# One PSUM tile with a free list, and the key steps of 15 units scored in three groups instead of four

## The chip, the cores and the metric

The kernel runs on one core of a Trainium2 chip. The metric is the device time of one execution in microseconds (us). Three runs of the kernel before took 412.25, 418.48 and 414.56 us; the median is 414.56 us. The profile is one execution of the same program, taken by the hardware profiler.

Names used below: PE is the matrix engine (TensorE), PEld its weight loads, ACT the scalar engine, DVE the vector engine, POOL the GpSimd engine, SP the engine that issues most DMAs. PSUM is the memory of eight banks into which PE writes its results; ACT and DVE read them out.

## The reference

```
q_n, k_n = rmsnorm(q, g_q), rmsnorm(k, g_k)       # 8 batches x 12 heads x 448 x 64
scores   = (q_n @ k_n^T) / 8
attn     = exp(scores - rowmax) ; attn /= rowsum + 1e-9
x        = (attn @ v) as 3584 tokens x 768
h        = x @ w_in                                # 768 x 2048
out      = max(0.01 h, h) @ w_out                  # 2048 x 768
```

## The kernel before, in words

**Units.** The attention is done in 24 units `u`; one unit is four heads of one batch, so three units make a batch. The 448 keys of a unit are cut into seven key steps of 64. For one key step `t`, `score` (line 196) issues four 64x64 matmuls with 448 columns, two for each of two PSUM banks. Such a pair of banks is a *slot* (`slot`, line 193). `ex` (line 209) then empties the slot with one ACT instruction, the exponential of 128x896 scores (line 218), into the tile `et`, from which the sums and the product with `v` are taken (`zcol`, line 299; `pv`, line 360).

**Stages of a unit.** The main loop (lines 982 to 1073) gives each unit from 3 on four stages, `d` = 0 to 3. At the start of a stage `qk` (line 202) scores the steps of `STEPS[d]`: step 0, then 1 and 2, then 3 and 4, then 5 and 6. In stage 0 there follow the row maximum on DVE (`shift_max`), the product with `v` and the sums of the unit before (`pv_slot`, `zcol`), a small matmul and DVE work that give the exponent's shift (`shift_mm`, lines 243 to 257), a copy of the product out of PSUM (`pv_out`, line 316, called `x` in the profile), and the logarithm of the sums (`zcol_ln`, line 327). `ex` comes right behind the scores in stages 1 to 3.

**Items.** The rest of each stage is filled by `fill` (line 756) with items of the two dense layers, taken from a queue. `PLAN` (line 745) says how many for each unit and stage, mostly two or three. An item `moe1` (line 385) is six matmuls of 128x128 with 448 columns into one bank `hps`, which ACT empties with the leaky ReLU (line 383). Items of the second layer (`moe2`, line 425, and `seven`, line 480) are eight matmuls of 384 columns, mostly emptied by DVE. After each item `fill` calls one of the stage's `jobs`: loads, normalisation of later units, squares for the unit three ahead (`prep_sq`, line 148, on ACT in stage 3), and the like. Each engine executes its own instructions in the order in which the program lists them (`manual_schedule`); engines wait for each other by semaphores.

**PSUM.** The eight banks are two pools: two slots of two banks (tag `sT`), and four single banks (tag `aux`) handed out in turn. `hold` and `drop` (lines 62 to 69) turn the four single banks into a list for the last two batches; in the tail two more banks join it (line 646). Slots hold the scores, the product with `v`, and some sums; single banks hold the results of items, the sums of `zcol`, and transposes.

**Ends.** Units 0 to 2 are written out by hand before the loop (lines 786 to 980), units 22 and 23 carry the last batches' items (`late1`, line 605), and a tail after the loop (lines 1074 to 1084) runs what is left in the queue.

Of the kernel before, what the change touches and what calls it, by code (L numbers as in the profile page):

```python
# [18 lines left out]
def kernel(  # L19
# [34 lines left out]

    held = []

    def aux(shape, dtype, name):
        if held:
            return held[0].pop(0)
        return psum.tile(shape, dtype, tag="aux", bufs=4, name=name)  # L60

    def hold():
        if not held:
            banks = [psum.tile([P, 512], FP32, tag="aux", bufs=4, name=f"bank{i}") for i in range(4)]
            held.append(banks)

    def drop(bank):
        if held:
            held[0].append(bank)

# [96 lines left out]
    def prep_norm(u, c=ALL, tis=BOTH):  # L167
        n = c[1] - c[0]
        for ti in tis:
# [3 lines left out]
                buf(u, "rinv")[:, ti, :, c[0]:c[1], None].broadcast_to([P, 2, n, D]), op=ALU.mult)  # L173

    def prep_tr(u, ti, copies):
        tp = aux([P, NS, P], FP16, "tp")
        for (lo, hi), copy in copies:
            for x in range(lo, hi):
                nc.tensor.transpose(tp[:, x, :], buf(u, "n16")[:, ti, x].rearrange("p a d -> p (a d)"), ident16)
            copy(buf(u, "qkT")[:, ti, lo:hi], tp[:, lo:hi], ti == 0)  # L180

    def prep_trd(u):
# [7 lines left out]
    def kT(u, r, a, t):  # L190
        return buf(u, "qkT")[64 * a:64 * a + 64, 1, t, 64 * r:64 * r + 64]

    def slot():
        return psum.tile([P, 2, 512], FP32, tag="sT", bufs=2, name="sT")

# [12 lines left out]

    def ex(u):
        s = st[u]  # L210
        if "et" not in s:
            s["et"] = epool.tile([P, NS, 2, S], FP16, tag="et", name="et")
        for t, sT in s["sT"]:
            if isinstance(sT, list):
                for a in range(2):
                    nc.scalar.activation(s["et"][:, t, a], sT[a][:, 0:S], AF.Exp, bias=s["eb"], scale=1.0)
            else:
                nc.scalar.activation(s["et"][:, t], sT[:, :, 0:S], AF.Exp, bias=s["eb"], scale=1.0)  # L218

    def score0(u):  # L220
        banks = [aux([P, 512], FP32, "s0") for a in range(2)]
        score(u, 0, banks)
        st[u]["sT"] = [(0, banks)]
# [16 lines left out]
    def shift_bank(u):  # L240
        st[u]["pb"] = aux([P, 512], FP32, "pb")

    def shift_mm(u):
        s = st[u]
        if u > 0 and "pslot" in st[u - 1]:
            pb = st[u - 1]["pslot"][:, :, S:S + 64]
            for x in range(2):
                nc.tensor.matmul(pb[:, x], onesp, s["dg"][:, 64 * x:64 * x + 64], start=True, stop=True)
            nc.vector.tensor_reduce(s["spare"][:, 510:511], pb, axis=AXL.XY, op=ALU.max)  # L249
        else:  # L250
            if "pb" not in s:
                shift_bank(u)
            pb = s["pb"]
            nc.tensor.matmul(pb[:, 0:P], onesp, s["dg"], start=True, stop=True)
            nc.vector.tensor_reduce(s["spare"][:, 510:511], pb[:, 0:P], axis=AXL.X, op=ALU.max)
        s["eb"] = small.tile([P, 1], FP32, tag="eb", name="eb")
        nc.vector.tensor_scalar(s["eb"], s["spare"][:, 510:511], -1.0, DELTA, op0=ALU.mult, op1=ALU.add)
# [41 lines left out]
    def zcol(u):  # L299
        s = st[u]  # L300
        s["zc"] = aux([P, 512], FP32, "zc")
        ets = z_tiles(u)
        for i, e in enumerate(ets):
            for y in range(2):
                for a in range(2):
                    c = 32 * (2 * y + a)
                    nc.tensor.matmul(s["zc"][c:c + 32, 0:HS], onesr, e[:, a, HS * y:HS * y + HS],  # L307
                                     start=(i == 0), stop=(i == len(ets) - 1))
# [7 lines left out]
    def pv_out(u):  # L316
        s = st[u]
        s["x32"] = zpool.tile([P, 2, S], FP32, tag="x32", name="x32")
        if u in (3, 4, 5, 6):
            nc.vector.tensor_copy(s["x32"], s["pslot"][:, :, 0:S])  # L320
        else:
            nc.scalar.copy(s["x32"], s["pslot"][:, :, 0:S])  # L322

    def zcol_ln(u):
# [24 lines left out]
    def zinv(u):  # L349
        s = st[u]  # L350
        s["rz"] = zpool.tile([P, 2, S], FP32, tag="rz", name="rz")
        if "zslot" in s:
            nc.scalar.activation(s["rz"], s["zslot"][:, :, 0:S], AF.Ln)
            nc.scalar.activation(s["rz"], s["rz"], AF.Exp, bias=0.0, scale=-1.0)
        else:
            for r in range(2):
                nc.scalar.activation(s["rz"][:, r], s["zt"][r][:, 0:S], AF.Ln)
                nc.scalar.activation(s["rz"][:, r], s["rz"][:, r], AF.Exp, bias=0.0, scale=-1.0)

    def pv(u, t0=0, t1=NS):  # L360
        s = st[u]
        if t0 == 0 and "pslot" not in s:
            s["pv"] = [aux([P, 512], FP32, "pv") for r in range(2)]
        for t in range(t0, t1):
            for r in range(2):
                for a in range(2):
                    nc.tensor.matmul(s["pv"][r][64 * a:64 * a + 64, 0:S], vts[u % NV][64 * r:64 * r + 64, a, t],  # L367
                                     s["et"][64 * r:64 * r + 64, t, a], start=(t == 0), stop=(t == NS - 1))
# [16 lines left out]
    def moe1(b, ft):  # L385
        xt = xts[b]
        hps = aux([P, 512], FP32, "hps")
        for kt in range(KT):
# [36 lines left out]
    def moe2(pair, t, half, part, late=False, cut=8):  # L425
# [3 lines left out]
        if part == 0:  # L429
            ost[1] = aux([P, 512], FP32, "op2")  # L430
        op2 = ost[1]
# [48 lines left out]
    def seven(pair, tt, nxt=None, last=False, mixed=False):  # L480
# [6 lines left out]
        def bank(name):  # L487
            g[name] = aux([P, 512], FP32, name)
            return g[name]
# [115 lines left out]
    def late1(b, tail, after):  # L605
# [32 lines left out]
        def get(n, s):  # L638
            g[n, s] = aux([P, 512], FP32, "hp")
            return g[n, s]  # L640

        def start():
            hold()
            if tail:
                for i in range(2):
                    drop(slot()[:, 0])
            for name in ("u", "v"):
# [52 lines left out]
    def push(b):  # L700
# [32 lines left out]
        else:  # L733
# [13 lines left out]
            "3232", "2222", "3323", "3232", "2322", "4356", "5232")  # L747
    STEPS = ((0,), (1, 2), (3, 4), (5, 6))

    def narrow(u):  # L750
# [35 lines left out]
    with tc.manual_schedule():  # L786
# [5 lines left out]
        load(2)  # L792
        gps = aux([P, 512], FP32, "gps")
        wbank = aux([P, 512], FP32, "warm")
        warm(32, wbank)
# [9 lines left out]
        prep_rinv(0, (0,))  # L805
        nc.vector.tensor_copy(gcol, gps[:, 0:1])
        prep_ssq(0, ALL, (1,))
        prep_rinv(0, (1,))
# [5 lines left out]
        def tr(u, ti, chunks, tp=None):  # L814
            if tp is None:
                tp = aux([P, NS, P], FP16, "tp")
            for c, copy in chunks:
                for x in range(*c):
                    nc.tensor.transpose(tp[:, x, :], buf(u, "n16")[:, ti, x].rearrange("p a d -> p (a d)"), ident16)
                copy(buf(u, "qkT")[:, ti, c[0]:c[1]], tp[:, c[0]:c[1]], ti == 0)  # L820
            return tp

        tr(0, 0, ((CA, acopy),))
        tr(0, 0, ((CB, acopy),))
        tpk = tr(0, 1, ((K0, vcopy),))
        warm(6, wbank)
        prep_sq(1, ALL, (0,))
        qk(0, STEPS[0])
        shift_max(0)
        tr(0, 1, ((K1, acopy),), tpk)  # L830
        prep_sq(1, ALL, (1,))
# [8 lines left out]
        warm(10, st[0]["pb"])  # L840
        shift_mm(0)
        prep_ssq(1)

# [19 lines left out]
        load_w_in(1024, 1024)  # L863
        wb = aux([P, 512], FP32, "warm")
        warm(12, wb)
        qk(0, (2,))
        ex(0)
        warm(8, wb)
        qk(0, (3,))
        ex(0)  # L870
        tr(1, 0, ((ALL, vcopy),))
        tpk = tr(1, 1, ((K0, vcopy),))
# [6 lines left out]
        shift_max(1)  # L879
        vcopy(*k1[0])  # L880
        shift_bank(1)
        qk(0, (5,))
# [24 lines left out]
        qk(1, (2,))  # L907
        warm(6, st[1]["pb"])
        ex(1)
        trn(2, 0, vcopy)  # L910
# [36 lines left out]
        trn(3, 0, vcopy)  # L947
        warm(8, st[2]["pb"])
        trn(3, 1, vcopy)
        xmul(1)  # L950
        prep_ssq(4, ALL, (1,))
        qk(2, (4,))
        ex(2)
        st[2]["zt"] = [aux([P, 512], FP32, "zt") for r in range(2)]
        zsum(2, 0, 3)
# [22 lines left out]
        for ft in range(2):  # L978
            prelu(0, gt[:, ft, 0:S], first[:, ft, 0:S])
        del queue[0:2]  # L980

        for u in range(3, NU):
            for d in range(4):
                if d > 0 or u > 3:
                    qk(u, STEPS[d])
                    if d == 0:
# [9 lines left out]
                        else:  # L996
# [3 lines left out]
                            zinv(u - 1)  # L1000
                    ex(u)
                    if d == 0 and narrow(u - 1):
# [7 lines left out]
                def job(fn, *args):  # L1010
                    jobs.append(lambda: fn(*args))

                if d == 0:
                    if u == 3:
# [98 lines left out]
```

## Time and profile before

| what | value |
|---|---|
| median of three runs | 414.56 us (412.25 to 418.48) |
| span of the profiled execution, first to last instruction | 410.6 us |
| its own time | not listed apart; the nearest run shown is 412.25 us, 1.6 us over the span |
| PE matmuls busy | 398.2 us (97%), 3840 |
| ACT busy | 298.4 us (73%), 470 |
| DVE busy | 307.2 us (75%), 490 |
| exponentials of one slot (line 218) | 166, 1010 ns each, 159.6 us |
| matmuls of the scores into slots (line 199) | 664 |

A line of a group or of the timeline reads: start, duration, engine, line, operation, `output<-inputs`, shape, how many. Matmuls are pipelined, so a row of twelve matmuls ends a little after the next row has begun; distances between starts are the measure. "issue" as the end of a wait means that the engine waited for nothing that the profile shows.

### The profile page before, as it was taken

Reading aid. Unit: us, or ns where it says so; the run is one execution under the profiler, and the core shown is the slowest. Engines: PE = TensorE matmul, PEld = TensorE weight load, DVE = VectorE, ACT = ScalarE, POOL = GpSimd, SP = SyncE. Lnnn points to the kernel's source line nnn. Section 1 sums busy time; section 2 is a strip of 40 time slices with the busy share of each in tenths; the row PEclk is TensorE's granted clock in tenths of the full one; section 3 lists DMA queues with packets and bytes.
Section 4 is the critical chain, followed back from the end, with each engine's and each line's share of the span. In section 5 each row is a group of like instructions: output and inputs, shape, how many; then the busy total and the mean of one; then the engine's idle time right before and its main releaser. Section 6 shows DMA issues by size and latency. Waiting matters only on the chain.

```text
span 410.6 us, 9395 instructions
## 1 busy us (share of the span) xinstructions
PE 398.2 (97%) x3840; PEld 219.7 (54%) x3840; DVE 307.2 (75%) x490; ACT 298.4 (73%) x470; POOL 69.1 (17%) x70
## 2 busy tenths in 40 slices
PE   8689999999999999999999999999999999999996
PEld 7455444454445544555445544455445557558963
DVE  5997789999788766767669667678568788658772
ACT  5998977677887699777986779967986657653600
POOL 1886433100020200020020200003001202000000
PEclk9999999999999999999999999999999999999999
DMA  5999999999565885577666896667662460032014
GB/s 192 264 255 253 232 234 236 232 190 200 136 156 95 232 224 106 149 196 169 155 151 77 216 201 143 164 127 170 196 114 46 121 152 17 7 80 77 2 44 111
DMA packets 72526, 62.87 MB, mean 153 GB/s; under 512 B 36388, under 2 KB 67620, under 8 KB 72484
## 3 DMA queue, kind: packets, MB, share of 16 engines
q1 hardware_dynamic: 61888, 50.08, 47.6%
q0 software_dynamic: 10272, 11.80, 18.4%
q8 instruction: 30, 0.49, 0.5%
q10 hardware_dynamic: 324, 0.39, 0.3%
q14 instruction: 12, 0.10, 0.1%
HBM read 45.61 MB, written 11.01 MB: 138 GB/s over the span
## 4 chain that ended last, share of the span: by engine, by line
PE 90%; DVE 4%; ACT 3%; DMA 1%; issue 1%; SPq 0%; DVEq 0%
PE hps L389 28%; PE sT L199 10%; PE sT L367 6%; PE op L435 6%; PE mc L485 5%; PE ma L485 5%; PE bank L485 5%; PE md L485 5%; PE bank L617 5%; PE zc L307 3%; PE mb L485 3%; ACT et L218 2%; PE sT L485 2%; PE bank L435 1%; DVE n L171 1%; DMA rk<-in_k_dram 1%
## 5 line engine op out<-in xcount | busy, mean ns | idle before, releaser
L218 ACT ACTIVATE et<-sT,eb 128x896 f16<-128x896 f32 x166 | 159.6, 1010 | 25.8 <-PE sT L199 13.5
L389 PE MATMUL hps<-xt,win 128*128 128x448 f16 x600 | 120.8, 353 | 0.0
L389 PEld LDWEIGHTS <-win 128*128 128x128 f16 x612 | 56.7, 98 | 57.9 <-issue 9.9
L383 ACT ACTIVATE gt<-hps 128x448 f16<-128x448 f32 x100 | 53.9, 558 | 3.8 <-PE hps L389 3.2
L199 PE MATMUL sT<-qkT 64*64 64x448 f16 x664 | 52.3, 363 | 4.0 <-ACT et L218 3.2
L159 DVE TENSOR_REDUCE ssq<-sq 128x14 f32<-128x896 f32 (+2 forms) x49 | 50.2, 1057 | 0.8 <-ACT sq L148 0.8
L485 PEld LDWEIGHTS <-sa 128*128 128x128 f16 x352 | 32.8, 98 | 26.0 <-issue 5.8
L128 POOL DMA_DIRECT2D vt<-in_v_dram x24 | 17.9, 746 | 166.4 <-PE sT L367 166.0
L322 ACT COPY x<-sT 128x896 f32<-128x896 f32 x16 | 14.5, 907 | 29.8 <-DVE sT L249 27.5
L199 PEld LDWEIGHTS <-qkT 64*64 64x64 f16 x672 | 15.4, 104 | 37.2 <-issue 32.5
L485 PEld LDWEIGHTS <-gt 128*128 128x128 f16 x264 | 25.3, 98 | 18.4 <-issue 2.1
L347 POOL TENSOR_TENSOR xt<-x,rz 128x896 f16<-128x896 f32 x9 | 19.5, 2170 | 80.8 <-DMA rz<-zs 73.5
L236 DVE TENSOR_REDUCE sT<-sT 128x1 f32<-128x896 f32 x22 | 24.1, 1096 | 11.4 <-PE sT L199 11.3
L367 PE MATMUL sT<-et,vt 64*64 64x448 f16 x560 | 29.9, 349 | 0.0
L171 DVE TENSOR_TENSOR n<-rq,rinv 128x896 f16<-128x896 f32 (+2 forms) x25 | 26.3, 1055 | 3.2 <-ACT rinv L165 3.2
L435 PE MATMUL op<-wout,gt 128*128 128x384 f16 x160 | 28.4, 327 | 0.0
L171 DVE TENSOR_TENSOR n<-rk,rinv 128x896 f16<-128x896 f32 (+2 forms) x26 | 27.5, 1065 | 0.0
L292 DVE TENSOR_TENSOR ea<-ea,et 128x896 f16<-128x896 f16 x25 | 15.6, 625 | 15.2 <-ACT et L218 14.3
L367 PEld LDWEIGHTS <-vt 64*64 64x64 f16 x672 | 20.3, 107 | 10.6 <-issue 0.4
L435 PEld LDWEIGHTS <-gt 128*128 128x128 f16 x192 | 17.7, 98 | 13.8 <-issue 3.2
L485 PE MATMUL ma<-wout,gt 128*128 128x384 f16 x128 | 23.5, 326 | 0.0
L292 DVE TENSOR_TENSOR ea<-et 128x896 f16<-128x896 f16 x14 | 9.4, 672 | 11.9 <-ACT et L218 11.9
(144 smaller groups left out, 548.4 us busy)
## 6 DMA issues: line engine op xcount, KB each, us to landing
rq<-in_q_dram SPq DMA_DIRECT2D x24, 448.0 KB, 3.9
rk<-in_k_dram SPq DMA_DIRECT2D x24, 448.0 KB, 4.9
out_dram<-ost SPq DMA_DIRECT2D x52, 192.0 KB, 3.5
rz<-zs SPq DMA_DIRECT2D x80, 112.0 KB, 2.3
vt<-in_v_dram POOLq DMA_DIRECT2D x24, 224.0 KB, 5.2
win<-in_moe_w_in_dram POOLq DMA_DIRECT2D x8, 384.0 KB, 14.3
wout<-in_moe_w_out_dram POOLq DMA_DIRECT2D x2, 1536.0 KB, 28.9
out_dram<-ost SPq DMA_DIRECT2D x4, 96.0 KB, 2.1
```

The lines of the kernel that those rows point to most:

```text
L159: nc.vector.tensor_reduce(buf(u, "ssq")[:, ti, :, c[0]:c[1]], buf(u, f"sq{ti}")[:, :, c[0]:c[1]], axis=AXL.X, op=ALU.add)
L171: nc.vector.tensor_tensor(buf(u, "n16")[:, ti, c[0]:c[1]].rearrange("p s a d -> p a s d"), src[:, :, c[0]:c[1]], buf(u, "rinv")[:, ti, :, ...
L199: nc.tensor.matmul(banks[a][64 * r:64 * r + 64, 0:S].rearrange("p (t x) -> p t x", t=NS), kT(u, r, a, t), qT(u, r, a), start=True, stop=True)
L218: nc.scalar.activation(s["et"][:, t], sT[:, :, 0:S], AF.Exp, bias=s["eb"], scale=1.0)
L236: nc.vector.tensor_reduce(s["spare"][:, 511:512], sT[:, :, 0:S], axis=AXL.XY, op=ALU.max)
L292: nc.vector.tensor_tensor(s["ea"], s["et"][:, 0] if t == 1 else s["ea"], s["et"][:, t], op=ALU.add)
L367: nc.tensor.matmul(s["pv"][r][64 * a:64 * a + 64, 0:S], vts[u % NV][64 * r:64 * r + 64, a, t], s["et"][64 * r:64 * r + 64, t, a], start=(t ...
L383: nc.scalar.activation(dst, src, AF.Prelu, bias=0.0, scale=1.0, alpha=0.01)
L389: nc.tensor.matmul(hps[:, 0:S], win16[:, kt // 2, kt % 2, ts(ft, P)], xt[:, kt // 2, kt % 2], start=(kt == 0), stop=(kt == KT - 1))
L435: nc.tensor.matmul(op2[:, 0:HC], gt[:, ft, ds(col(t), P)], wout16[:, ft, ds(HC * half, HC)], start=(i == 0), stop=(i == FT - 1))
L485: nc.tensor.matmul(bank[:, 0:HC], a[:, f], b[:, f], start=(first and f == 0), stop=(f == HF - 1), skip_group_check=not first)
L617: nc.tensor.matmul(bank[:, HX * i:HX * i + HX].rearrange("p (t x) -> p t x", t=NS), w, x[:, kt], start=start, stop=(kt == HK - 1), skip_gr ...
```

## The change

All of PSUM becomes one tile `banks` of eight banks. `aux` hands out single banks and `slot` pairs of neighbouring banks from one list `free`; `drop` gives a bank or a pair back when the program has listed its last reader, and it goes to the end of the list. Up to unit 6 the list is still parted: banks 0 to 3 single, banks 4 to 7 as two pairs. From unit 7 on (`shared`) any two free neighbours can become a slot, and `aux` takes, of all free banks but the one given back last, the first whose neighbour is in use. The same list serves the tail.

Units 7 to 21 (`tripled`) score their key steps as 0; 1, 2, 3; none; 4, 5, 6 in the four stages. `ex(u, 2)` empties the first two slots at once; the third exponential becomes the first job of the stage, so it stands behind the first item on ACT, and the stage's other jobs move back by one item. `PLAN` and the queue of items are as before.

```diff
-    held = []
-    def aux(shape, dtype, name):
-        if held:
-            return held[0].pop(0)
-        return psum.tile(shape, dtype, tag="aux", bufs=4, name=name)
...
-    def slot():
-        return psum.tile([P, 2, 512], FP32, tag="sT", bufs=2, name="sT")
+    banks = psum.tile([P, 8, 512], FP32, tag="banks", name="banks")
+    single = [banks[:, i] for i in range(8)]
+    double = [banks[:, 2 * i:2 * i + 2] for i in range(4)]
+    free = [3, 0, 2, 1, 4, 5, 6, 7]
+    shared = []
+    def mine(i):
+        return shared or i < 4
+    def aux():
+        can = [i for i in free if mine(i)]
+        if shared:
+            can = [i for i in can[:-1] if i ^ 1 not in free] or can
+        free.remove(can[0])
+        return single[can[0]]
+    def slot():
+        if shared:
+            can = [i for i in free if i ^ 1 in free]
+            last = {i // 2: n for n, i in enumerate(free) if i in can}
+        else:
+            last = {i // 2: n for n, i in enumerate(free) if i >= 4 and i ^ 1 in free}
+        x = min(last, key=lambda i: last[i])
+        for i in (2 * x, 2 * x + 1):
+            free.remove(i)
+        return double[x]
...
-    def ex(u):
+    def ex(u, most=NS):
...
-        for t, sT in s["sT"]:
+        for t, sT in s["sT"][:most]:
...
                 nc.scalar.activation(s["et"][:, t], sT[:, :, 0:S], AF.Exp, bias=s["eb"], scale=1.0)
+                drop(sT)
+        s["sT"] = s["sT"][most:]
...
+    TRIPLES = ((0,), (1, 2, 3), (), (4, 5, 6))
+    def tripled(u):
+        return 7 <= u < NU - 2
...
+                if u == 7 and d == 0:
+                    shared.append(u)
                 if d > 0 or u > 3:
-                    qk(u, STEPS[d])
+                    qk(u, (TRIPLES if tripled(u) else STEPS)[d])
...
-                    ex(u)
+                    ex(u, 2)
...
+                if st[u]["sT"]:
+                    job(ex, u)
```

The other edits put a `drop` behind each last reader (`pv_out`, `zinv`, the transposes and warm-up matmuls of the hand-written part) and call `aux()` without shape and name.

## The prediction

> **What bounds the kernel now.** I began with the busy times and the 40 slices.
>
> ```profile
> span 410.6 us, 9395 instructions
> PE 398.2 (97%) x3840; PEld 219.7 (54%) x3840; DVE 307.2 (75%) x490; ACT 298.4 (73%) x470; POOL 69.1 (17%) x70
> PEclk9999999999999999999999999999999999999999
> ```
>
> PE is busy all the way at its full granted clock; ACT and DVE have a quarter to spare. The chain that ended last lies 90% on PE. So the time goes down only if PE does less or loses less between its pieces, and goes up by whatever PE is made to wait. The waits tell which of its losses are left:
>
> ```profile
> PEld L199 <- issue: 32.5, 92, 0.8
> ...
> PE sT L199 <- ACT et L218: 3.2, 7, 0.7
> ```
>
> The scores wait for an exponential 3.2 us in all, nearly all of it in the hand-written start: from 36 us on it is one wait of 0.4 us. But 92 times a score group's first weight load stands about 0.35 us with nothing to wait for. Those are the places where PE goes from 128x128 matmuls to the 64x64 matmuls of the scores. How much of it is lost is read from the timeline; here PE in unit 10:
>
> ```profile
> 146.01 0.57 PE L199 MATMUL sT<-qkT 64*64 64x448 f16 x8
> 146.51 3.58 PE L389 MATMUL hps<-xt,win 128*128 128x448 f16 x18
> 150.02 0.57 PE L199 MATMUL sT<-qkT 64*64 64x448 f16 x8
> 150.53 2.44 PE L389 MATMUL hps<-xt,win 128*128 128x448 f16 x12
> 152.90 0.57 PE L199 MATMUL sT<-qkT 64*64 64x448 f16 x8
> 153.41 2.44 PE L389 MATMUL hps<-xt,win 128*128 128x448 f16 x12
> 155.78 0.38 PE L199 MATMUL sT<-qkT 64*64 64x448 f16 x4
> ```
>
> From item to item, 18 matmuls and a group take 150.53 - 146.51 = 4.02 us, 12 and a group 153.41 - 150.53 = 2.88. Six matmuls are thus 1.14 (0.19 each), and a group of two steps costs 2.88 - 12 x 0.19 = 0.60. A key step itself costs 0.57 - 0.38 = 0.19 (eight matmuls against four). Two steps are 0.38, so each **group loses 0.22 us** in going to 64x64 and back.
>
> **What goes.** Units 7 to 21 have one group less in stages 1 to 3 (the group of stage 0 runs straight into the product with v, also 64x64). Fifteen groups at 0.22 are **3.3 us off PE**. Its matmuls remain; so do the counts on ACT and DVE, and SP and POOL list the same instructions in the same order, so no load, store or transpose is passed by anything new on its queue. Bounds: 0 if three steps in a row cost the 0.22 in another way; 15 x 0.35 = 5.3 if all of the issue wait were lost.
>
> [...]
>
> **What is added: waits for banks.** Three steps need six of the eight banks at once. The order of the built program shows which reader each new pair waits for. Within the loop all are per bank: no wait covers the whole tile. In stage 1 the first pair waits for the copy x, the second for the exponential of step 0, as before. The third is new. It waits for the first two leaky ReLUs of stage 0 in units 7, 8, 11, 14, 17, 20; for the logarithm and the first of them in 10, 13, 16, 19; for the logarithm, with or without a DVE copy, in 9, 12, 15, 18, 21. Whether that is late is read from ACT in unit 10:
>
> ```profile
> 144.24 0.91 ACT L322 COPY x<-sT 128x896 f32<-128x896 f32 x1 [2.27 <-DVE sT L249]
> 145.04 1.01 ACT L218 ACTIVATE et<-sT,eb 128x896 f16<-128x896 f32 x1
> 145.94 0.36 ACT L327 ACTIVATE zs<-zc 128x224 f32<-128x224 f32 x1
> 146.18 0.56 ACT L383 ACTIVATE gt<-hps 128x448 f16<-128x448 f32 x1
> ```
>
> The third step would start 0.38 after the group, at 146.39; the ReLU ends at 146.74. **Units 10 and 16** (only two items in stage 0) wait 0.35, with the signal some 0.4: 0.8 us together. Behind it on PE stands everything else, so it counts in full. With three items PE comes a whole item later: in unit 11 the second ReLU ends at 161.73 and the third step would start at 161.49 + 0.38 = 161.87; unit 8: 114.98 against 115.02; unit 14: 209.37 against 209.41. Those just fit. In units 12 and 18 the logarithm ends about 0.05 late: 0.1 together.
>
> **What moves on ACT.** In stage 3 a third exponential (0.95) stands behind the first item's ReLU and ahead of the two squares (0.96 each). Everything ACT does up to the next unit's copy x ends up to 0.95 later; PE comes only 0.19 later. What covers it is the idle time ahead of that copy:
>
> ```profile
> ACT x L322 <- DVE sT L249: 27.5, 15, 3.9
> ```
>
> By unit it is 0.72 (unit 8), 2.03, 2.27, 0.38 (unit 11), 2.56, 2.27, 1.18 (unit 14), 2.31, 2.27, 0.38 (unit 17), 2.56, 2.27, 1.18, 2.03. Only 8, 11 and 17 are short: by 0.95 - 0.19 less the idle, 0.04, 0.38 and 0.38. Some of that comes back because stage 2 has no exponentials now and ACT reaches stage 3 free of queue: step 4 could begin about 0.3 earlier than the 153.70 of unit 10. I take 0.15 in each of the three, **0.45 us** (0 to 1.1). If that cover is gone, the copy, the next exponential and both ReLUs slip together, and the third step of stage 1 is what is late next.
>
> The product with v needs step 6 last. In unit 10 the third exponential would end near 156.8 and the last matmuls that read it start about 157.5: it fits by 0.7. The third group of stage 3 waits for readers of stage 2, which ACT, without exponentials there, serves at once; I take nothing (a ReLU late each time would be 0.56). Inside the stages the banks come back from the two early exponentials, one or two items ahead of need. DVE's additions of exponentials and its sums of squares shift by an item, with a stage to spare.
>
> **The tail** has eight banks instead of six, but `aux` may take a fresh one. Two items of the last batch now use the bank whose ReLU was issued two items before, where the old list gave an older one. The ReLU (`gt<-bank`) starts at 378.12 and ends at about 378.68, and the item that would now use its bank starts at 378.50: 0.25 with the signal; at 385.40 the same costs 0.2. Together **0.45 us**. Units 0 to 6, 22 and 23 keep their groups, and the readers they wait for end before PE comes: nothing.
>
> **Sum** on the profiled execution: -3.3 + 0.8 + 0.1 + 0.45 + 0.45 = -1.5, a span of 409.1 for 410.6. That execution lies 1.6 under the fastest run and 4.0 under the median; I carry the difference over to the median: 414.56 - 1.5 = **413.1 us**.
>
> **Rivals.**
> 1. *Full gain.* PE slips by the first waits, ACT catches up, and the free list spares the tail: -3.3 or, with part of the wider issue bound, -4, 410.6 to 411.3. For it: single waits of 0.04 to 0.4 are small against ACT's idle quarter. Against: the waits of units 10 and 16 come from the DVE result that starts the copy, and no slack elsewhere moves it.
> 2. *No change.* The loss recurs, for instance because the third step's matmuls don't follow without a gap, 0.22 x 15 given back: with the waits, about +1.8, or 416.4; if the waits are absent too, 414.6. Against: 28 matmuls with v in a row keep 0.19 for each four.
> 3. *Slower: ACT becomes the bound at each unit's start.* The place is the third pair of stage 1. If it waits on average half a ReLU-and-signal more than I find in all fifteen units, say 0.5 each, the cost is 7.5 + 0.45 - 3.3 = +4.7, 419.2 us. It decides from 0.2 us a unit on, where waits eat the 3.3. Beyond 2% (+8.3) it takes 0.75 a unit, that is ACT late by its whole 0.95 everywhere. For it: margins of 0.04 in units 8, 14 and 20. Against: idle of over 2 us ahead of the copy in nine of the units.
>
> **Chances.** The forecast, -3 to 0: 0.57. Full gain: 0.18. No change up to +2: 0.12. Slower by more than that: 0.13, of which 0.04 beyond 2%. Two per cent, 8.3 us, is about what a measurement of this kernel tells from no change, and a gain of that size has no source in PE's 0.22 a group: 0.02. The range leaves out most of the slower case and adds the scatter of a median of runs that lie 6 us apart: 410 to 418.
>
> **What would show it.** Right: 15 fewer score groups; groups of twelve matmuls spaced about 0.8 from item to item; the issue wait on the score loads down by some 5 us; PE's waits at score groups near 1.5 us, in units 10 and 16 above all. Wrong: PE waiting for a ReLU or an exponential in most units' stage 1 or 3, an ACT with no idle time ahead of the copy x, or a lost 0.22 that reappears inside the twelve.

## The result

| | before | after |
|---|---|---|
| median | 416.52 us (412.25 to 418.86, four runs) | 433.0 us (432.63 to 433.88, four runs) |
| ratio, with its 95% interval | | 1.0456 (1.0397 to 1.0514) |
| span of the profiled execution | 410.6 us | 431.4 us |
| its own time | not listed apart | 433.22 us, 1.8 over its span |

The ratio counts fast runs alone, so it is not the quotient of the two medians (1.040): two of the four runs before, at 418.48 and 418.86 us, took over 1.5% longer than the fastest. By it the change made the kernel slower by 4.6%; 413.1 us had been forecast. The page of the kernel after answers the first question, whether PE is still busy all the way:

```profile
span 431.4 us, 9408 instructions
...
PE 404.2 (94%) x3840; PEld 225.1 (52%) x3840; DVE 310.5 (72%) x490; ACT 300.2 (70%) x470; POOL 68.9 (16%) x70
...
PEclk9899999999979999999997999999996999999999
```

It is not. PE is idle for 6% of the span (3% before), its matmuls take 6 us longer in all although their number is the same, and the granted clock has four dents where there were none. The waits of the same kernel (engine and line, what it waited for: total us, times, longest) say who keeps it waiting. In this kernel line 222 is the score matmul, 242 the exponential, 414 the leaky ReLU, 497 and 500 the sums `s1` and `s2`, 516 the matmuls of `seven`, 538 the copy of `ma`:

```profile
PEld L222 <- issue: 29.6, 83, 0.8
...
DVE sa L497 <- ACT gt L414: 18.7, 3, 6.7
...
PE banks L516 <- DVE ost L538: 7.8, 3, 2.8
...
PE banks L516 <- DVE sa L500: 6.2, 3, 2.1
...
PE banks L222 <- ACT et L242: 3.3, 8, 0.6
```

The scores are not at fault: their issue wait fell from 32.5 to 29.6 us, and they wait 3.3 us for exponentials, nearly what they did before (3.2). What is new are three waits of about 2.1 us and three of 2.2 to 2.8 us, PE standing at `seven` for DVE. They are in three units only. To place them I took, unit by unit, the start of the first sum matmul of `zcol` (`zc<-et,onesr`, now `banks<-et,onesr`) in both timelines, and from one such mark to the next the difference, after minus before:

| stretch | difference, us |
|---|---|
| start to unit 4 | +1.26 |
| units 4 to 6 | 0.00 |
| unit 7, 9, 11, 13, 15, 17, 19, 21 | -0.22, -0.22, -0.23, -0.24, -0.24, -0.24, -0.23, -0.23 |
| units 12, 18 | -0.16, -0.17 |
| units 10, 16 | +0.21, +0.23 |
| **units 8, 14, 20** | **+6.84, +7.68, +6.53** |
| unit 22 | +0.01 |
| the rest, units 23 and tail | +0.23 |

The first row is not the change's: in the runs below the same stretch lies between +0.2 and +1.7 us, and in this one the clock is at half from 17.7 to 21.1 us, in the hand-written start. Units 8, 14 and 20 lose 21.05 us together; everything else gives back about 1.5. The whole result is in three units.

These are the units of the tripled ones that have `ADDED` equal to 3, and the loop treats them alike: stage 1 has, after the job `prep_g`, one composite job of two sums of squares (`prep_ssq`, `ssq` in the rows) and two additions of exponentials (`add_e`, `ea`). DVE in unit 8 of the kernel before (start, duration, engine, line, operation, form, count, and in brackets the idle time ahead of it and what ended that):

```profile
112.71 0.45 DVE L155 TENSOR_SCALAR qkT<-qkT,gcol 128x896 f16<-128x896 f16 x1
113.07 2.08 DVE L159 TENSOR_REDUCE ssq<-sq 128x14 f32<-128x896 f32 x2
116.34 0.62 DVE L292 TENSOR_TENSOR ea<-et 128x896 f16<-128x896 f16 x1 [1.20 <-ACT et L218]
117.24 0.62 DVE L292 TENSOR_TENSOR ea<-ea,et 128x896 f16<-128x896 f16 x1 [0.28 <-ACT et L218]
118.20 0.43 DVE L466 TENSOR_TENSOR sa<-gt 128x512 f16<-128x512 f16 x1 [0.33 <-ACT gt L383]
118.66 0.43 DVE L469 TENSOR_TENSOR sa<-sa,gt 128x512 f16<-128x512 f16 x1
119.00 0.55 DVE L507 COPY ost<-ma 128x384 f32<-128x384 f32 x1
119.47 1.85 DVE L472 TENSOR_TENSOR sa<-gt 128x512 f16<-128x512 f16 x1
```

and in the same unit of the kernel after:

```profile
113.76 0.45 DVE L176 TENSOR_SCALAR qkT<-qkT,gcol 128x896 f16<-128x896 f16 x1
120.04 2.29 DVE L497 TENSOR_TENSOR sa<-gt 128x512 f16<-128x512 f16 x1 [5.83 <-ACT gt L414]
122.36 0.43 DVE L500 TENSOR_TENSOR sa<-sa,gt 128x512 f16<-128x512 f16 x1
122.70 2.07 DVE L180 TENSOR_REDUCE ssq<-sq 128x14 f32<-128x896 f32 x2
124.69 0.62 DVE L320 TENSOR_TENSOR ea<-et 128x896 f16<-128x896 f16 x1
125.34 0.62 DVE L320 TENSOR_TENSOR ea<-ea,et 128x896 f16<-128x896 f16 x1
125.88 0.55 DVE L538 COPY ost<-banks 128x384 f32<-128x384 f32 x1
```

Three things are different. First, the order: the composite job came one place later. In unit 8 the item in between is the first of `seven`, which puts `s1` and `s2` on DVE's list; in units 14 and 20 stage 1 has only two items, and a job that is left over comes behind what the end of the stage lists, which is `s1` and `s2` again. So `ssq` and `ea`, which could have run in the 5.83 us of idle time, now stand behind `s1`, which waits for ACT, and ahead of the copy of `ma`. Second, `s1` starts late; why is on ACT:

```profile
118.07 0.60 ACT L414 ACTIVATE gt<-banks 128x448 f16<-128x448 f32 x1
118.50 1.08 ACT L242 ACTIVATE et<-banks,eb 128x896 f16<-128x896 f32 x1
119.39 0.62 ACT L414 ACTIVATE gt<-banks 128x448 f16<-128x448 f32 x1
```

The third exponential, 1.08, lies between the two leaky ReLUs of the stage, and `s1` needs the second. Third, `s1` takes 2.29 in place of 0.43. POOL runs its product of x and 1/z just then:

```profile
119.98 2.06 POOL L376 TENSOR_TENSOR xt<-x,rz 128x896 f16<-128x896 f32 x1 [7.28 <-DMA rz<-zs]
```

In the kernel before the same product fell on `s3` (the row at 119.47: 1.85 in place of 0.41), which nothing waited for. PE in the same unit shows what follows:

```profile
115.66 0.78 PE L222 MATMUL banks<-qkT 64*64 64x448 f16 x12
116.37 2.44 PE L420 MATMUL banks<-xt,win 128*128 128x448 f16 x12
118.65 1.46 PE L516 MATMUL banks<-wout,gt 128*128 128x384 f16 x8
119.95 0.81 PE L516 MATMUL banks<-tw,sa 128*128 128x384 f16 x4
122.84 0.82 PE L516 MATMUL banks<-tw,sa 128*128 128x384 f16 x4 [2.08 <-DVE sa L500]
126.49 2.72 PE L516 MATMUL banks<-wout,gt 128*128 128x384 f16 x8 [2.82 <-DVE ost L538]
129.14 1.33 PE L222 MATMUL banks<-qkT 64*64 64x448 f16 x12
```

PE waits for `s2`, then, after four matmuls, for the copy, and then its matmuls are slow: eight take 2.72 where 1.46 is usual, and twelve of the scores 1.33 in place of 0.78. By distances between starts, against the 0.65 of four matmuls, 1.39 of eight ahead of a score group and 0.70 of twelve scores that undisturbed rows have, unit 8 loses 2.24 at the first wait, 3.00 at the second and 1.82 to the slow matmuls, less the 0.22 gained: 6.84. Units 14 and 20 are split in the same way (in unit 20 the first four matmuls behind the first wait are slow too, 1.43, but the second wait covers that). Over the three: **6.7 us at the first wait, 9.0 at the second, 6.0 to the clock**, less 0.7 gained.

So far this is read, not shown. The groups of three, the new list of banks and the order of jobs all changed at once.

### The profile page after: what moved, and what is told of

Its sections match the earlier page's. It is cut to its first block, busy times and chain, and to the rows that moved or that the text cites. A ratio compares the mean times of both kernels' runs of the same rounds, so it can differ in the third digit from the quotient of the medians.

```text
span 431.4 us, 9408 instructions
## 1 busy us (share of the span) xinstructions
PE 404.2 (94%) x3840; PEld 225.1 (52%) x3840; DVE 310.5 (72%) x490; ACT 300.2 (70%) x470; POOL 68.9 (16%) x70
## 4 chain that ended last, share of the span: by engine, by line
PE 76%; ACT 10%; DVE 7%; DMA 4%; issue 1%; POOL 0%; SPq 0%; ACTq 0%; DVEq 0%; POOLq 0%
PE banks L516 22%; PE banks L420 22%; PE banks L222 8%; PE banks L466 7%; PE banks L398 6%; PE banks L648 6%; ACT et L242 6%; PE banks L335 2%; ACT gt L414 2%; DVE sa L497 2%; DMA rq<-in_q_dram 1%; DVE ssq L180 1%; DMA qkT<-n 1%; DMA rk<-in_k_dram 1%; DMA out_dram<-ost 1%
## 5 line engine op out<-in xcount | busy, mean ns | idle before, releaser
L242 ACT ACTIVATE et<-banks,eb 128x896 f16<-128x896 f32 x166 | 160.6, 1015 | 27.3 <-PE banks L222 14.8
L420 PE MATMUL banks<-xt,win 128*128 128x448 f16 x612 | 122.2, 353 | 0.0
L414 ACT ACTIVATE gt<-banks 128x448 f16<-128x448 f32 x104 | 56.8, 566 | 5.8 <-PE banks L420 4.6
L222 PE MATMUL banks<-qkT 64*64 64x448 f16 x672 | 52.7, 375 | 3.9 <-ACT et L242 3.3
L516 PE MATMUL banks<-tw,sa 128*128 128x384 f16 x264 | 48.9, 333 | 6.2 <-DVE sa L500 6.2
L523 DVE TENSOR_TENSOR ost<-banks,ost 128x384 f32<-128x384 f32 x55 | 30.5, 554 | 21.7 <-PE banks L516 20.2
L516 PE MATMUL banks<-wout,gt 128*128 128x384 f16 x176 | 36.2, 353 | 7.8 <-DVE ost L538 7.8
L516 PEld LDWEIGHTS <-gt 128*128 128x128 f16 x264 | 26.5, 102 | 28.5 <-issue 13.4
L398 PE MATMUL banks<-et,vt 64*64 64x448 f16 x672 | 37.0, 349 | 0.1
L222 PEld LDWEIGHTS <-qkT 64*64 64x64 f16 x672 | 18.1, 107 | 35.6 <-issue 29.6
L466 PE MATMUL banks<-wout,gt 128*128 128x384 f16 x192 | 34.1, 327 | 0.0
L262 DVE TENSOR_REDUCE banks<-banks 128x1 f32<-128x896 f32 x22 | 24.1, 1097 | 10.3 <-PE banks L222 10.3
```

Source lines behind the costliest of these rows:

```text
L222: nc.tensor.matmul(banks[a][64 * r:64 * r + 64, 0:S].rearrange("p (t x) -> p t x", t=NS), kT(u, r, a, t), qT(u, r, a), start=True, stop=True)
L262: nc.vector.tensor_reduce(s["spare"][:, 511:512], sT[:, :, 0:S], axis=AXL.XY, op=ALU.max)
L414: nc.scalar.activation(dst, src, AF.Prelu, bias=0.0, scale=1.0, alpha=0.01)
L420: nc.tensor.matmul(hps[:, 0:S], win16[:, kt // 2, kt % 2, ts(ft, P)], xt[:, kt // 2, kt % 2], start=(kt == 0), stop=(kt == KT - 1))
L466: nc.tensor.matmul(op2[:, 0:HC], gt[:, ft, ds(col(t), P)], wout16[:, ft, ds(HC * half, HC)], start=(i == 0), stop=(i == FT - 1))
L516: nc.tensor.matmul(bank[:, 0:HC], a[:, f], b[:, f], start=(first and f == 0), stop=(f == HF - 1), skip_group_check=not first)
```

## The experiments

The theory: the change's third exponential, put in as first job, reorders DVE in units 8, 14 and 20, and the rest follows from that. Rival A: three key steps in a row make PE wait for ACT. Rival B: the one PSUM tile with its list makes PE wait for banks. "Steps" are the differences of the table above. The ratios are to runs of the kernel before that were taken beside each experiment; their medians are 413.8 to 414.3 us.

### e1_order_back: the order on DVE restored

```diff
-                if st[u]["sT"]:
+                with_g = d == 1 and u in (8, 14, 20)
+                if st[u]["sT"] and not with_g:
                     job(ex, u)
...
-                if d == 1 and 5 <= u < NU - 1:
+                if with_g:
+                    job(lambda u: (ex(u), prep_g(u + 1)), u)
+                elif d == 1 and 5 <= u < NU - 1:
                     job(prep_g, u + 1)
```

> The changed kernel, but in stage 1 of units 8, 14 and 20 the third exponential shares one job with the scaling of q for the next unit, so that the sums of squares and the additions of exponentials stand on DVE ahead of the sums s1 and s2 again, as in the kernel before; groups, list of banks and everything else stay. Theory (the order on DVE in three units): the steps of units 8, 14 and 20, +6.8, +7.7 and +6.5 us against the kernel before, become about -0.2 each like their neighbours'; the span is near 408.5 us, or 409.7 if the clock dips at the start of the kernel again, and the ratio to the kernel before is 0.990 to 0.999. Rival A (three steps in a row make PE wait for ACT's exponentials and leaky ReLUs): the groups stay, so the loss stays, a span of 428 to 432. Rival B (PSUM as one tile with a list makes PE wait for banks): it stays too, 428 to 432.

Measured: a span of 415.4, 419.07 us, ratio 1.0116 (1.0084 to 1.0149). The steps of the three units are +2.04, +2.00 and +2.00. 15 of the 21 us are the order on DVE with the clock behind it, and both rivals lose most of their ground; but the theory's -0.2 did not come. The second wait is gone, the first is as long as ever. DVE of this kernel in unit 8:

```profile
118.98 2.29 DVE L497 TENSOR_TENSOR sa<-gt 128x512 f16<-128x512 f16 x1 [1.14 <-ACT gt L414]
```

and PE, at its full clock:

```profile
121.79 0.82 PE L516 MATMUL banks<-tw,sa 128*128 128x384 f16 x4 [2.08 <-DVE sa L500]
```

What I had taken for one cause is two: the exponential between the leaky ReLUs still makes `s1` late (118.98 for 118.20 before, PE being level), and POOL still runs beside it. That the clock stays full is one execution's, the fastest of the six runs (417.13 to 421.77); how its waits lay is told in the last section.

### e2_list_only: the PSUM tile and its list alone

```diff
-        return 7 <= u < NU - 2
+        return False
```

> The changed kernel with the four groups (0, 1-2, 3-4, 5-6) everywhere: only the one PSUM tile and its list of banks are left of the change. Theory: no job is shifted, so units 8, 14 and 20 take what they took before; a span of 410.5 to 411.5, ratio 0.997 to 1.003. Rival A: the same. Rival B: the loss is here, some 7 us in each of units 8, 14 and 20, a span near 430.

Measured: a span of 411.6, 414.54 us, ratio 0.9992 (0.9962 to 1.0022); from unit 4 to unit 22 no step differs by more than 0.07, and unit 23 with the tail takes 0.24 more. Rival B falls as the cause of the 21 us: with the old groups the list costs next to nothing, and what it costs is at the end.

### e3_shift_only: the order of the jobs in the kernel before

```diff
+                if d == 1 and u in (8, 14, 20):
+                    jobs.append(lambda: None)
                 if d == 1 and 5 <= u < NU - 1:
                     job(prep_g, u + 1)
```

> The kernel before, with an empty job put first in the list of stage 1 of units 8, 14 and 20 and nothing else: DVE's two sums of squares and two additions of exponentials move behind s1 and s2 there, no instruction is added on any engine, PSUM and the groups are as before. Theory: each of the three units loses 6 to 7.5 us, the span is 429 to 433, ratio 1.04 to 1.055. Rivals A and B: the groups and the banks are those of before, so 410 to 412 and a ratio of 0.997 to 1.003.

Measured: a span of 420.9, 423.73 us, ratio 1.0209 (1.0158 to 1.0261). Steps of +3.73, +3.73 and +2.16, all others behind the start within 0.03. An empty job in three places, with no instruction added, costs about 10 us: the order alone is enough for a loss, without a group or a bank of the change. The size was missed, because here the exponential does not lie between the leaky ReLUs: `s1` starts at 118.87 and is done before POOL starts, so the first wait is absent and only the second remains, 1.99 in each unit. In unit 8:

```profile
118.87 0.42 DVE L466 TENSOR_TENSOR sa<-gt 128x512 f16<-128x512 f16 x1 [5.04 <-ACT gt L383]
...
123.45 2.30 PE L485 MATMUL ma<-wout,gt 128*128 128x384 f16 x8 [1.99 <-DVE ost L507]
```

Why the same 1.99 costs 3.73 twice and 2.16 once is told in the last section.

### e5_warm: PE kept busy during the waits

```diff
             fn = queue.pop(0)[1]
+            if u in (8, 14, 20) and d == 2 and n < 2:
+                bank = aux()
+                warm(36, bank)
+                drop(bank)
             fn()
```

> The changed kernel with 36 matmuls of 128x128 into a free bank, about 2 us of PE time, ahead of the first and of the second item of stage 2 in units 8, 14 and 20: they fill PE's two waits there (2.08 for s2 and 2.82 for the copy of ma in unit 8) and wait for nothing themselves. Nothing that PE waits for comes sooner. Theory, the waits open the loss and the granted clock of about 0.5 for 6 us behind them adds some 1.8 us of it: the clock stays near 1.0, the waits are hidden but their ends stay where they are, and each of the three units loses 4.7 to 5.5 us instead of 6.5 to 7.7; a span near 426. If the lower clock costs nothing by itself, the three losses stay where they are, a span of 431.

Measured: a span of 424.8, one run of 426.91 us. The granted clock stays at 1.00 throughout. Steps of +5.01, +3.81 and +5.02 in place of +6.84, +7.68 and +6.53: with 4.0 us of idle matmuls added in each unit, it is still 7.2 us faster there. The clock is a loss of its own; unit 8, where nothing else differs, gains 1.83, and 1.82 had been read from the distances. Two units tell about POOL by accident. In unit 14 the transfer that POOL waits for came later, POOL started at 219.30 when `s1` (218.27) was over, and `s1` took 0.42; that is why 3.81 is less than expected, and some 1.2 of the 7.2 us; without it 6.0 are left. In unit 18 POOL's product fell on the product `n` on DVE, which took 2.81 in place of 1.08, and PE waited 0.92 for an addition behind it.

### e6_ex_last: the third exponential behind the second leaky ReLU

```diff
-                if st[u]["sT"]:
+                if st[u]["sT"] and not (d == 1 and u in (8, 14, 20)):
                     job(ex, u)
...
-                            job(lambda u: (prep_ssq(u + 2), add_e(u)), u)
+                            job(lambda u: (ex(u), prep_ssq(u + 2), add_e(u)), u)
```

> The first experiment (DVE's order back) with one step more: in stage 1 of units 8, 14 and 20 the third exponential stands on ACT behind the second leaky ReLU of the stage, not between the two. Theory now: of the 2.0 us that each of these units still lost, the first cause is that exponential of 1.07, which let the last leaky ReLU end at 118.95 in place of 118.16 (unit 8), so that s1 on DVE started at 118.98, together with POOL's product x times 1/z (118.92), and took 2.29 in place of 0.42. With the order back s1 starts near 118.2 and ends before POOL starts: no wait of PE, the three steps become -0.2 each, a span of 408.3 to 409.7, ratio 0.991 to 0.998. Rival: the groups of three steps cost the 2.0 by themselves, whatever the order on ACT: a span near 415, ratio 1.01.

Measured: a span of 411.3, 413.18 us, ratio 0.9975 (0.995 to 1.0). The step of unit 8 is -0.18, as expected; those of units 14 and 20 are +0.83. The place of one exponential was worth 2.2 and twice 1.2 us. In units 14 and 20 something else now shows, which the larger waits had covered. DVE in unit 14:

```profile
213.68 1.84 DVE L503 TENSOR_TENSOR sa<-gt 128x512 f16<-128x512 f16 x1
215.44 0.41 DVE L506 TENSOR_TENSOR sa<-gt,sa 128x512 f16<-128x512 f16 x1
215.78 1.08 DVE L192 TENSOR_TENSOR n<-rq,rinv 128x896 f16<-128x896 f32 x1
216.78 0.55 DVE L523 TENSOR_TENSOR ost<-banks,ost 128x384 f32<-128x384 f32 x1
```

and PE:

```profile
217.38 0.81 PE L516 MATMUL banks<-tw,sa 128*128 128x384 f16 x4 [0.99 <-DVE ost L523]
```

PE's matmuls of `mc` wait for the addition of `mb`. In the program `mc` is given the bank that `mb` has just held. No free bank stands without a free neighbour there, so the list hands out its oldest entry, and that is `mb`'s: two banks are held by the third key step, and the other five have been given back later still, four by exponentials and one by `ma`. The old pool handed `mc` a third bank, which the scores had nothing to do with. So the shared list has a price after all, 1 us in each of two units, once the scores ask for six banks at a time and the addition stands behind `s3` and `n`, as it does in these two units.

### e4_pool_only and e7_pool_later: POOL's product listed later

Both make this edit, e4 in the changed kernel, e7 in e1.

```diff
-                if d == 1 and narrow(u - 1) and not 5 <= u < 8 and ADDED.get(u, 0) < 4:
+                if d == 1 and narrow(u - 1) and not 5 <= u < 8 and ADDED.get(u, 0) < 4 and u not in (8, 14, 20):
                     xmul_pool(u - 1)
+                if d == 3 and u in (8, 14, 20):
+                    xmul_pool(u - 1)
```

> The changed kernel as it is (third exponential first, DVE's order of the changed kernel) with POOL's product of units 7, 13 and 19 moved from stage 1 to stage 3 alone. Theory: s1 takes 0.42, so PE's wait of 2.08 for s2 shrinks to 0.1 to 0.3 and everything behind it on DVE comes 1.87 earlier; but sums of squares and additions (3.3 us together) still stand ahead of the copy of ma, so the second wait stays near 2.8. Each of the three units loses 2.6 to 3.2, or up to 4.7 where the clock falls behind the one long wait; a span of 416.5 to 422. If the order on DVE alone were the loss, nothing would change (431).

> The first experiment (DVE's order back, the third exponential still between the two leaky ReLUs) with POOL's product x times 1/z of units 7, 13 and 19 moved from stage 1 to stage 3 of units 8, 14 and 20. Theory: s1 still starts 0.8 late at 118.98 but takes 0.42, s2 ends near 119.8, PE's fifth matmul of mb waits 0.1 to 0.3 in place of 2.08, and the three steps are between -0.2 and +0.2; a span of 408.3 to 410.5. If the exponential's order is the loss and POOL is not, s1 stays long and the steps stay +2.0, a span near 415; what POOL delays in stage 3 instead shows in the same steps.

Measured: spans of 430.2 (one run of 431.96 us) and 417.2 (419.01 us, ratio 1.0097, 1.0064 to 1.013); the steps stay at +6.29, +7.42, +6.38 and at +2.03, +2.01, +2.03. The edit did nothing at all: POOL in e7 ran its product when its transfer had landed, as before.

```profile
120.49 2.06 POOL L376 TENSOR_TENSOR xt<-x,rz 128x896 f16<-128x896 f32 x1 [7.28 <-DMA rz<-zs]
```

Listing an instruction later moved nothing here, because POOL had nothing else listed in between (its next row in e7 starts at 130.83). The runs say nothing on POOL's share; as repeats they show how steady the losses are.

### e10_no_pool: the product on DVE, in e1

```diff
-                if d == 1 and narrow(u - 1) and not 5 <= u < 8 and ADDED.get(u, 0) < 4:
+                if d == 1 and narrow(u - 1) and not 5 <= u < 8 and ADDED.get(u, 0) < 4 and u not in (8, 14, 20):
...
                         if u > 3:
                             job(prep_trd, u + 2)
+                        if u in (8, 14, 20):
+                            job(xmul_sb, u - 1)
```

> The first experiment (DVE's order back, the third exponential between the two leaky ReLUs) with the product x times 1/z of units 7, 13 and 19 given to DVE, behind its two products n in stage 2 to 3 of units 8, 14 and 20, so that POOL computes nothing beside s1. Theory (s1 is long because POOL runs beside it): s1 starts as late as before, at 0.8 behind, but takes 0.42 in place of 2.29; PE's wait of 2.08 shrinks to 0.1 to 0.3, the three steps turn from +2.0 to between -0.15 and +0.3; a span of 408.3 to 410.5, ratio 0.991 to 1.001. If s1 were long for another reason (its place behind a wait, its source just written), it stays 2.29 and the steps stay +2.0 or more.

Measured: a span of 411.3, 412.14 us, ratio 0.9958 (0.9931 to 0.9986). Steps of +0.17 in all three units. DVE in unit 8, with the same wait ahead of `s1` as in e1:

```profile
120.41 0.43 DVE L497 TENSOR_TENSOR sa<-gt 128x512 f16<-128x512 f16 x1 [1.14 <-ACT gt L414]
```

and PE:

```profile
121.35 0.82 PE L516 MATMUL banks<-tw,sa 128*128 128x384 f16 x4 [0.21 <-DVE sa L500]
```

So POOL's product beside it is what makes `s1` long, 1.87 us of PE's 2.08. The exponential's place alone costs 0.21 of idle PE and about 0.4 in the step (+0.17 in place of -0.22); beyond that it mattered because it moved `s1` into POOL's way.

### e9_plan and e12_add_first: the two remaining waits

e9 is e6 with three items in stage 0 of units 10 and 16 and two in stage 1; e12 adds one line that puts the addition of `mb` ahead of the product `n` in units 14 and 20.

```diff
-            "2322", "3232", "2222", "3323", "3232", "2322", "2322",
+            "3222", "3232", "2222", "3323", "3232", "2322", "3222",
...
             fn()
+            if u in (14, 20) and d == 2 and n == 1:
+                flush()
```

> The same kernel as the one with the exponential behind the leaky ReLU, and in units 10 and 16 three items in stage 0 and two in stage 1 in place of two and three. Theory: the waits of some 0.44 us that these two units have for the first leaky ReLU of stage 0 go, their steps turn from +0.2 to -0.2; a span 0.8 to 0.9 below that of its sibling, 407.4 to 408.9, ratio 0.989 to 0.997.

> The kernel with the exponential behind the leaky ReLU and three items in stage 0 of units 10 and 16, and in units 14 and 20 the addition of mb stands on DVE ahead of the product n in place of behind it. Theory for the +0.83 that these two units still lose: with six banks in the scores' hands the matmuls of mc get the bank that mb has just held, and wait 0.99 for its addition, which stands behind s3 (1.84 beside POOL) and n (1.08). With the addition first it ends 1.08 earlier, mc finds its bank free, and the steps of units 14 and 20 become -0.2: a span 2.1 below that of the kernel without this step, 407.4 to 409.3, ratio 0.988 to 0.995. If PE waits there for something else, the steps stay +0.8.

Measured: e9 has a span of 411.3, 412.5 us, ratio 0.9956 (0.9935 to 0.9976). The steps of units 10 and 16 turn from +0.21 and +0.22 to -0.23 and -0.22, as expected; the span is that of e6 only because the start took 0.94 us longer in the profiled execution. e12 has 409.4, 410.88 us, ratio 0.9939 (0.991 to 0.9967), and the steps of units 14 and 20 turn from +0.82 and +0.83 to -0.17: the wait was for that addition, and it is gone.

### e13_dve_mul: the best version

e9 with the edit of e10.

> The kernel with the exponential behind the leaky ReLU and three items in stage 0 of units 10 and 16, and the product x times 1/z of units 7, 13 and 19 on DVE (1.08) in place of POOL. Theory: s3 takes 0.42 in place of 1.84, so the addition of mb in units 14 and 20 ends 1.4 earlier although it still stands behind n, and mc does not wait: steps of -0.2 there, as with the addition moved; the 1.08 more on DVE is taken from its idle time ahead of the next addition. A span of 407.4 to 409.8, ratio 0.988 to 0.997.

Measured: a span of 408.5, 410.23 us, ratio 0.9907 (0.9872 to 0.9943). Every unit from 7 to 21 now has a step of -0.16 to -0.24, 3.29 us in all. With three small repairs (the exponential's place, which also puts DVE's order back, the plan, and the product on DVE) the change is a gain of about 1%, faster than both kernels, though by less than the 2% that I had set as the mark.

## Why the prediction was wrong, step by step

- **The gain of a group**: forecast 0.22 us for each of fifteen. Right. Where nothing else is in the way the steps are -0.22 to -0.24, and e13 has 3.29 / 15 = 0.22.
- **Units 10 and 16**: forecast 0.4 each, from a leaky ReLU that ends after PE wants its bank. Right: +0.21 and +0.23 in place of -0.22, 0.44 each, and gone when PE comes an item later (e9).
- **Units 12 and 18**: forecast 0.1 together, measured 0.07 and 0.06. Right, net of the 0.07 that the list alone gains there (e2).
- **ACT late in units 8, 11 and 17**: forecast 0.15 each. It did not happen: units 11 and 17 have -0.23 and -0.24, and unit 8 has -0.22 in e13. No run shows what made it up. The 0.95 of an exponential, from which the 0.15 was estimated, is what ACT shows: two in a row take 1.90 (unit 10 of the kernel before, at 153.70).
- **The tail**: forecast 0.45, measured 0.23 for unit 23 and the tail together, half of it. It is the list's, not the groups': e2 has 0.24 there.
- **The step that failed** was given one sentence and no price: "DVE's additions of exponentials and its sums of squares shift by an item, with a stage to spare." There was a stage to spare for those additions and sums themselves. But the shift took them past two other instructions on the same queue, `s1` and `s2`, and set them ahead of a third, the copy that PE waits for. Order on an engine that works in order is not slack: behind an `s1` that waits for ACT, 3.3 us of work had to be done before a copy that had been needed at once. It cost 9.0 us of waits, and the 6.0 us of clock went with them when e1 removed 15.0; how far the first wait would have lowered the clock by itself is not shown: in e1 and e7, which keep that wait, the clock stayed at 1.00 through the three units.
- **A term that was missing**: in stage 3 I had asked what the third exponential delays on ACT, but in stage 1 I looked only at banks. There it delayed the last leaky ReLU by 0.8 us, `s1` with it, and into POOL's product: 6.7 us (in unit 8 e6 removes all of its share, 2.2, and e10 all but 0.4).
- **"Inside the stages the banks come back ... ahead of need"**: not for `mc` in units 14 and 20, 0.99 each (e6, e12). In the changed kernel the larger waits hid it.
- **The rivals**: the slower one, ACT as the bound at each unit's start, named the wrong engine and the wrong place; the third pairs of stage 1 cost 1 us in all (0.88 and 0.13), where it had put 7.5. It put 0.04 on a loss beyond 2%.
- **Two readings of the prediction**: the matmuls with v were said to keep 0.19 for each four; by the starts of its own rows it is 1.43 / 7 = 0.20. And of its signs the issue wait on the score loads fell by 2.9 us, not by some 5, though the groups are 15 fewer and follow at the forecast spacing.

The terms that were worked out add up well: -3.3 + 0.88 + 0.13 + 0.23 = -2.1. Adding 21.05 and the 0.66 not gained in the three units, and 1.26 at the start, gives +20.9 against the measured +20.8.

## What to carry to other kernels

When a change puts one job ahead of others in a list, write out the new order of every engine whose instructions move, and for each moved instruction name what it now stands behind and what now stands behind it; one stalled instruction charges the whole queue to whoever waits at its end (here `s1`, waiting for ACT, held 3.3 us of work back that stood ahead of PE's copy). A wait that is priced at nothing because of slack should be priced again with the queue stopped at the worst place, and a few special cases of a loop (here three units of 24) deserve as close a look as the common one. When a gain is lost, repair one cause at a time: each repair here uncovered the next wait, which the larger one had hidden.

## What the runs showed of the hardware

**Three DVE operations took longer beside POOL's product; those that read a PSUM bank did not.** `s1`, 128x512 in fp16, takes 0.42 us alone and 2.25 to 2.29 when it starts within 0.1 us after POOL's product of two tiles (2.06). `s3` starting 0.7 after it takes 1.84 (e6), and `n` of 1.08 takes 2.81 when it starts 0.2 after it (e5). Whenever it started, `sa` ends 0.28 to 0.29 behind POOL's end and `n` 0.95: it looks like waiting, not like sharing. Additions of a PSUM bank to `ost` beside such a product keep their 0.55 to 0.56 (in the kernel after at 144.26, POOL's product running from 143.12 to 145.20). Where DVE was first, POOL's product took longer: in the kernel after `n` starts at 291.67 and keeps its 1.09, and POOL's product, from 291.95, takes 2.76. I had read the 1.85 of `s3` in the kernel before and not asked who would stand there next.

**The stretches at half clock lie on a grid of 3.41 us.** I located the ends of the half-clock stretches from the granted clock in 1 us steps. All that end before the span does are 3.4 or 6.8 us long, and their starts within one execution lie whole multiples of 3.413 apart: in the kernel after 17.72, 123.54, 225.94 and 324.92, which are 31, 30 and 29 such steps. e3 has the same wait of 1.99 us three times, at three places in this grid. Its stretches of the grid (from:to, length, busy us of PE, PEld, DVE, ACT and POOL, granted clock, then DMA):

```profile
120.51:123.92 3.41, 1.42 (x9) 0.76 (x8) 3.38 (x7) 1.81 (x4) 1.19 (x1) 1.00 0.45 172
123.92:127.34 3.42, 3.42 (x18) 1.23 (x16) 2.61 (x4) 1.50 (x3) 0.00 (x0) 0.50 0.02 5
...
219.49:222.90 3.41, 1.42 (x9) 0.68 (x7) 3.38 (x7) 0.54 (x2) 0.36 (x1) 1.00 0.18 69
222.90:226.32 3.42, 3.42 (x17) 1.38 (x17) 1.78 (x3) 3.13 (x5) 0.00 (x0) 0.50 0.11 21
315.06:318.47 3.41, 2.68 (x16) 1.48 (x16) 3.29 (x5) 2.23 (x5) 2.11 (x1) 1.00 0.05 11
318.47:321.89 3.42, 2.16 (x18) 1.03 (x18) 3.39 (x8) 0.82 (x3) 0.00 (x0) 1.00 0.00 0
```

Twice the whole wait lies in one stretch, PE is busy for 1.42 of 3.41, and the next stretch runs at half clock; the third time the grid cuts the wait in two, PE is busy for 2.68 and 2.16, and the clock stays at 1.00. At a granted clock of 0.50, 3.42 us cost, as an estimate from that clock, 1.71 us of matmuls; the steps of 3.73 and 2.16 lie 1.57 apart. e7, whose grid is carried on in steps of 3.413 from a stretch at its start (16.82 to 23.64), has its three waits of about 2.05 us cut at 1.35, 1.13 and 0.65 us from their start, so that no stretch has more than 1.42 us of idle time, and its clock stays at 1.00 there. e1's grid, taken from where its clock falls behind the last matmuls, cuts its three waits as well: the longest idle time in one stretch is 1.65 us (117.94 to 121.36), and there too the clock stays at 1.00.

The idle time alone does not tell which stretch is followed by half clock. A stretch of e4 in unit 20 is idle for 1.83 us and the next one is at full clock; a stretch of e9 in the hand-written start, with many short matmuls, is idle for 1.37 and the next one is at half:

```profile
320.07:323.48 3.41, 1.58 (x10) 0.74 (x8) 2.53 (x2) 0.82 (x2) 2.06 (x1) 1.00 0.04 9
323.48:326.90 3.42, 0.82 (x4) 0.41 (x5) 3.39 (x6) 0.55 (x2) 0.00 (x0) 1.00 0.00 0
...
13.28:16.69 3.41, 2.04 (x26) 1.43 (x25) 3.41 (x5) 3.35 (x8) 3.41 (x5) 1.00 1.11 267
16.69:20.11 3.42, 2.90 (x25) 1.65 (x25) 3.00 (x6) 2.39 (x4) 3.42 (x6) 0.50 1.09 212
```

In these rows of the loop 1.83 us of idle time is followed by full clock and 1.99 by half, and in the start 1.37 by half; what is counted as busy is open. In the kernel after, unit 14 also shows a stretch at half clock with 1.1 us of idle time (225.94 to 229.35) that is followed by another at half clock, though a stretch at full clock with 1.26 us of it was followed by full clock (e3, 318.47 to 321.89). A stretch at half clock with 0.62 us of idle time was followed by full clock (e4, 125.51 to 128.92). Whether the phase of the grid is also behind the scatter of the runs was not tried.
